# Four of seven stage-1 groups of two batches take one shared maximum, raised on GpSimd, in an attention-and-gated-FFN kernel

## The chip, the cores and the metric

The kernel runs on one core of a Trainium2 chip. The metric is device time in microseconds (us) of one execution; less is better. Before the change three runs gave 723.48, 723.59 and 724.96 us, median 723.59 us.

## What is computed

For each of 4 batches, x has 12416 rows of 128 numbers. Stage 1 lets 32 inducing rows attend over all the rows of x, stage 2 lets every row of x attend over the 32 results h, and a gated feed-forward network (128 to 1536 to 128) follows.

```python
def mab(q, kv):
    s = scale * (q @ kv.transpose(0, 2, 1))
    s = s - s.max(-1, keepdims=True)
    a = np.exp(s)
    a /= a.sum(-1, keepdims=True) + 1e-09
    return a @ kv
h = mab(I, x)            # stage 1
y = mab(x, h)            # stage 2
gate = 1.0 / (1.0 + np.exp(-(y @ w_gate)))
out = (gate * (y @ w_val)) @ w_out
```

## The kernel before, in words

**Tiles.** A batch is 97 chunks of 128 rows. One chunk stands alone (group 6, "the single"), 96 make six groups of 16 (groups 0 to 5; `groups`, L48). Batches are numbered 0 to 3 here; "batches 3 and 4" of the change are numbers 2 and 3. The whole of x of a batch lies in SBUF twice, as it is (`xn`) and transposed (`xT`), each in two buffers that the batches use in turn. A batch's loads are issued by GpSimd (`x_load`, L73), its transposes are DMAs issued by SyncE (`x_transpose_dma`, L87).

**The feed-forward loop sets the pace.** Four chunks make a block of 512 rows, 97 blocks in all. The 12 slices of the hidden width are worked off in 8 steps per block, alternately two slices (even step) and one (odd step). Step t does: on TensorE the value fill v(t) and the gate fill g(t + 2) (`hidden_mm`, L847); on VectorE the product u(t) = (tanh + 1) * v (L891); on ScalarE tanh(t + 2) of the gate (`gate`, L872). The gate fill g(t + 2) uses the PSUM banks of g(t), so it waits for tanh(t); the value fill v(t) uses those of v(t - 2), so it waits for u(t - 2). Odd steps also run `project` (L912), the matmuls with `w_out`, usually 12, and once per block ScalarE copies the block's result out (L940). Each engine takes its instructions strictly in the order in which this loop writes them.

**Slots.** An even and an odd step are one slot (`t // 2`); a batch has 96 slots, and o is the slot at which a batch's blocks begin (`base`, L947). Everything else is written out by hand at slots: `at(slot, make)` puts a piece behind the even step, `late=True` behind the odd step (`beside`, L981). While the loop works on batch b, the slots of that batch hold most of stage 2 of batch b and stage 1 of batch b + 1:

- `plan_stage1` (L287), one group of batch b + 1: at slot `score` four matmuls into one PSUM bank and VectorE's maximum over it (L222); at `score + 1`, late, ScalarE's exp (L235) with the negated maximum as bias; at `score + 2` a DMA transpose of the weights; at the three slots of `total` the sum over the rows in two halves (L270, 32 matmuls in all, into PSUM) and ScalarE's copy of the sum into `hst` (L285). Each group keeps a maximum and a sum of its own.
- `plan_combine` (L376): at `lead` VectorE's minimum over the negated maxima (L384) and `join_min` (L355), eleven small GpSimd steps that end in `top`; at `weights` ScalarE's exp over the seven maxima with `top` as bias (L389, tile `w`); one slot later GpSimd's weighted sum of the seven group sums (`join`, L393); later h and its products with the gate and value matrices.
- `plan_stage2` (L577), one group: scores at `score` and `score + 1`, ScalarE's copy to SBUF at `take` (late, L480), then GpSimd's maximum by a tree of subtract, clamp, add (`s2_lower_pool`, L482; tiles `rise` and `top`); ScalarE's exp at `weigh` (late, L504); GpSimd's sum at `weigh + 1` (L512), reciprocal and spread to `a2n` at `weigh + 3` (L536 to L558); the DMA transpose to `a2r` at `weigh + 8` (L569), which the group's first fills read.

All scores, sums and the like of stages 1 and 2 use one PSUM bank in turn, tag "m": the next user's matmuls wait until the last reader of the one before has done.

For batches b = 1 and 2 as the loop has them (so stage 1 of batches 2 and 3), the slots before are, relative to o: scores of groups 0 to 5 at 8, 12, 24, 28, 40, 44 and of the single at 32; sums at 15/16, 18/19, 31, 35, 47/48, 50/51 and 43; the combine at 52 (`lead`) and 55 (`weights`).

Of the kernel before, what the change touches and what calls it, by code (L numbers as in the profile page):

```python
# [9 lines left out]
F32 = mybir.dt.float32  # L10
F16 = mybir.dt.float16
BF16 = mybir.dt.bfloat16
AF = mybir.ActivationFunctionType
ALU = mybir.AluOpType
AX = mybir.AxisListType

AFTER = mybir.DependencyInfo(mybir.DependencyClass.Sync, mybir.DependencyReason.DATA)
P = 128
GC = 16
BC = 4  # L20
NEG = 1.0e30
TINY = 1.0e-9 / P


@with_exitstack
def kernel(
# [9 lines left out]
    nc = tc.nc  # L36
    B, N, C = x.shape
    m = inducing.shape[0]
# [4 lines left out]
    NG = NCH // GC  # L43
# [43 lines left out]
    def x_transpose_dma(b, s):  # L87
        c0, n = groups[s]
        xT_tile(b)
        nc.sync.dma_start(  # L90
            xT[b][:, c0 : c0 + n, :],
            xn[b][:, c0 : c0 + n, :].rearrange("p j c -> p (j c)"),
            transpose=True,
        )
# [66 lines left out]
    arrival = [0, NG] + list(range(1, NG))  # L161
    at_col = {s: p for p, s in enumerate(arrival)}
    EARLY = NS - 3
    nml = const.tile([P, 1 + NS - EARLY], F32, tag="nml")
    l1l = const.tile([P, 1 + NS - EARLY], F32, tag="l1l")
    nm1s = [const.tile([P, NS], F32, name=f"nm1_{q}", tag=f"nm1_{q}") for q in range(2)]
# [23 lines left out]
    def at(slot, make, late=False):  # L190
        plan.setdefault((slot, late), []).append(make)


    def s1_col(b, s):
        p = at_col[s]
        if b == 0 and p >= EARLY:
            return nml, l1l, slice(1 + p - EARLY, 2 + p - EARLY)
        return nm1s[b % 2], None if b else l1s, slice(p, p + 1)
# [58 lines left out]
    def s1_turn_dma(b, s, a1T):  # L257
        a1 = s1p.tile([P, 4, P], F16, tag="a1")
        nc.sync.dma_start(a1[:], a1T[:], transpose=True)
        return a1  # L260

    def s1_sum_pe(b, s, a1, hp, k0, k1):
        c0, n = groups[s]
        ng, w, R = s1_dims(s)
        for k in range(k0, min(k1, w)):
            for cols, src in ((slice(0, C), None), (slice(C, C + 1), ones16[:])):
                for g in range(ng):
                    if b == 0 and src is not None:
                        continue
                    nc.tensor.matmul(  # L270
                        hp[32 * g : 32 * g + 32, cols],
                        a1[:, k, 32 * g : 32 * g + 32],
                        xn[b][:, c0 + g * w + k, :] if src is None else src,
                        start=(k == 0 and src is None),
                        stop=(k == w - 1),
                        skip_group_check=True,
                    )

    def s1_sum_keep(b, s, hp):
        ng, w, R = s1_dims(s)  # L280
        width = C + 1 if b else C
        summed[b] += 1
        if b == 0 and at_col[s] >= EARLY:
            return hp[:, 0:C]
        nc.scalar.copy(out=hsts[b % 2][0:R, at_col[s], 0:width], in_=hp[0:R, 0:width])  # L285

    def plan_stage1(b, s, score, total):  # L287
        st = {}
        full = groups[s][1] == GC

        def begin():
            st["s1"] = s1_score(b, s, "m")

        def weigh():
            st["a1T"] = s1_exp(b, s, st["s1"])

        def turn():
            if full:
                st["a1"] = s1_turn_dma(b, s, st["a1T"])
            else:  # L300
                st["a1"] = s1_turn_copy(s, s1_turn_pe(b, s, st["a1T"]))

        at(score, begin)
        at(score + 1, weigh, late=full)
        at(score + 2, turn)
        first, second, keep = total

        def part(k0, k1):
            if k0 == 0:
                st["hp"] = ps.tile([P, C + 1], F32, tag="m", name="hp_ps")  # L310
            s1_sum_pe(b, s, st["a1"], st["hp"], k0, k1)

        at(first, lambda: part(0, 2))
        at(second, lambda: part(2, 4))
        at(keep, lambda: s1_sum_keep(b, s, st["hp"]))


    hT16 = {}
# [2 lines left out]
    def add_tree(x, k, out=None):  # L321
        while k > 1:
            r = k // 2
            o = x[:, 0:r] if k > 2 or out is None else out
            nc.gpsimd.tensor_tensor(out=o, in0=x[:, 0:r], in1=x[:, k - r : k], op=ALU.add)
            k -= r
# [49 lines left out]
    def plan_combine(b, lead, weights, fill):  # L376
        q = b % 2
        nm1, hst = nm1s[q], hsts[q]
        st = {}

        def least():
            assert summed[b] == NS
            ml = bp.tile([P, 1], F32, tag="ml")
            nc.vector.tensor_reduce(out=ml[:], in_=nm1[:], axis=AX.X, op=ALU.min)  # L384
            st["col"] = join_min(bp, ml)

        def weigh():
            st["w"] = bp.tile([P, NS], F32, tag="w1", name="w1")
            nc.scalar.activation(  # L389
                out=st["w"][:], in_=nm1[:], func=AF.Exp, bias=st["col"][:], scale=-1.0  # L390
            )

        def join():  # L393
            hx = bp.tile([P, NS, C + 1], F32, tag="hx", bufs=1)
            nc.gpsimd.tensor_tensor(
                out=hx[:],
                in0=hst[:],
                in1=st["w"][:].unsqueeze(2).to_broadcast((P, NS, C + 1)),
                op=ALU.mult,
            )  # L400
            add_tree(hx, NS)
            e32l = bp.tile([P, m], F32, tag="e32l")
            nc.gpsimd.tensor_scalar(
                out=e32l[:],
                in0=e32[:],
                scalar1=hx[:, 0, C : C + 1],
                scalar2=TINY,
                op0=ALU.mult,
                op1=ALU.add,
            )  # L410
            st["hx"], st["e32l"] = hx, e32l

        def total():
            lh = ps.tile([P, 2, m], F32, tag="m", name="lh_ps")
            nc.tensor.matmul(lh[:, 0, :], ones[:], st["e32l"][:], start=True, stop=True)
            nc.tensor.matmul(lh[:, 1, :], st["hx"][:, 0, 0:C], e32[:], start=True, stop=True)
            st["lh"], st["li"] = lh, l_inverse(lh[:, 0, :])

        def part(hf):
            st["hw_ps"] = hw_fill(b, hf, "m")  # L420

        def keep(hf):
            if hf == 0:
                st["hwt"] = bp.tile([P, NI, P], F16, tag="hw", bufs=B, name="hwt")
            hw_take(st["hwt"], hf, st["hw_ps"])
            if hf == 1:
                hw[b] = st["hwt"]

        at(lead, least)
        at(weights, weigh)  # L430
        at(weights + 1, join)
        at(weights + 8, total)
        at(weights + 9, lambda: h_take(b, st["lh"][:, 1, :], st["li"]))
        for hf, (first, second) in enumerate(fill):
            at(first, lambda hf=hf: part(hf))
            at(second, lambda hf=hf: keep(hf), late=True)
# [511 lines left out]
    for b in range(B):  # L948
        o = base[b]
        more = b + 1 < B  # L950

        if b == 0:
            plan_stage2(0, groups[1][0], o, None, o + 3, soon=True)
            plan_stage2(0, groups[2][0], o + 5, o + 7, o + 18)
        for s in range(3 if b == 0 else 2, NG - 1):
            k = o + 16 * s - 28
            plan_stage2(b, groups[s][0], k, k + 2, k + (14 if more else 10))
        plan_stage2(b, groups[NG - 1][0], o + 56, o + 58, o + 66, far=o + 52)
        if not more:
            continue  # L960
        early = (
            [(9, (16, 17, 17)), (13, (23, 23, 23))]
            if b == 0
            else [(8, (15, 16, 17)), (12, (18, 19, 19))]
        )
        later = [(24, (31, 31, 31)), (28, (35, 35, 35)), (40, (47, 48, 49)), (44, (50, 51, 51))]
        for s, (score, total) in enumerate(early + later + [(32, (43, 43, 43))]):
            plan_stage1(b + 1, s, o + score, [o + e for e in total])
        plan_combine(b + 1, o + 52, o + 55, [(o + 72, o + 74), (o + 80, o + 82)])
        plan_stage2(b + 1, groups[0][0], o + 67, o + 70, o + 78)  # L970
        plan_stage2(b + 1, groups[1][0], o + 84, o + 86, o + 94)
        for g in range(NS):
            when = 3 * g if b else (5, 7, 17, 19, 22, 25, 20)[g]
            at(o + when, lambda b=b, g=g: x_transpose_dma(b + 1, g))
            if b == 0 and 3 <= g < NG:
                at(o + 12, lambda g=g: x_load(1, g))
        if b + 2 < B:
            for g in range(NG):
                at(o + (28 if b == 0 else 24, 33, 42, 60, 60, 82)[g], lambda b=b, g=g: x_load(b + 2, g))

    def beside(slot, late):  # L981
        for make in plan.pop((slot, late), ()):
# [53 lines left out]
```

## Time and profile before

| what | value |
|---|---|
| median of 3 runs | 723.59 us |
| the profiled execution's own time | 723.41 us |
| its span in the trace | 721.6 us |
| granted TensorE clock | 0.999 |
| GpSimd busy in the span | 420.3 us, 58% |
| maxima of stage 1 on VectorE, 128 x 512, batches 1 to 3 | 21, mean 681 ns |
| DMA | 65.21 MB, mean 90 GB/s |

The profile counts an engine as busy from the start of an instruction to its end; on VectorE and ScalarE the next one may start some 0.07 to 0.13 us before the end of the last, so that durations add up to more than the time that passes. What an instruction costs its engine is the distance from its start to the next one's start. The 1.8 us between the span and the execution's time are taken as fixed.

### The profile page before, as it was taken

What the parts mean: (1) busy time and instruction counts of PE and PEld (TensorE: products, weight loads), DVE (VectorE), ACT (ScalarE), POOL (GpSimd) and SP (SyncE); (2) the same over time, 40 slices, a digit from 0 to 9 for tenths busy, and PEclk for the clock granted to TensorE, in tenths of its full rate; (3) what the DMA queues carried; (4) which work ended last, traced back from release to release, by engine and by line L of the source; (5) the groups of instructions that cost most, each with busy time, mean ns of one, the idle gap of its engine ahead of it and who ended that gap; (6) DMA issues with size and microseconds to landing.
All of it is one profiled execution on the core that took longest, in us unless ns stands there. A gap on an engine that the chain in (4) does not pass through costs nothing.

```text
span 721.6 us, 21567 instructions
## 1 busy us (share of the span) xinstructions
PE 645.2 (89%) x8478; PEld 390.9 (54%) x8478; DVE 703.6 (98%) x871; ACT 674.2 (93%) x1008; POOL 420.3 (58%) x699
## 2 busy tenths in 40 slices
PE   7889889999998998999989988999999899898887
PEld 4555555555555555555555555555555555555555
DVE  4799999999999999999999999999999999999998
ACT  4699999999999999999999999999999999999996
POOL 4464753888653747588666366398856665636200
PEclk9999999999999999999999999999999999999999
DMA  8879935243668344236378432220232122121211
GB/s 172 171 138 171 181 82 109 74 90 76 89 131 164 78 104 93 57 81 127 60 119 154 100 76 61 58 75 31 76 74 59 45 60 69 51 60 45 62 45 46
DMA packets 116726, 65.21 MB, mean 90 GB/s; under 512 B 99824, under 2 KB 101008, under 8 KB 116624
## 3 DMA queue, kind: packets, MB, share of 16 engines
q1 hardware_dynamic: 111936, 49.81, 31.6%
q0 software_dynamic: 4416, 13.90, 10.8%
q8 instruction: 66, 1.08, 0.6%
q14 instruction: 36, 0.29, 0.2%
q10 hardware_dynamic: 272, 0.13, 0.1%
HBM read 27.80 MB, written 25.43 MB: 74 GB/s over the span
## 4 chain that ended last, share of the span: by engine, by line
DVE 53%; issue 22%; PE 13%; ACT 8%; DMA 2%; DVEq 1%; POOL 0%; ACTq 0%; POOLq 0%
DVE u L891 51%; ACT t L878 7%; PE acc_ps L922 6%; PE v_ps L859 5%; DMA xn<-in_x_dram 2%; DVE nm L222 2%; DVEq L891 1%; PE hp_ps L270 1%; PE g_ps L859 0%; POOL xn L81 0%; PE s_ps L210 0%; ACT hwt L351 0%; PE s_ps L443 0%; PE aT_ps L248 0%; ACT a1T L235 0%
## 5 line engine op out<-in xcount | busy, mean ns | idle before, releaser
L891 DVE SCALAR_TENSOR_TENSOR u<-t,v_ps 128x512 f16<-128x512 f16 (+1 forms) x778 | 675.0, 942 | 1.6 <-PE g_ps L859 0.7
L878 ACT ACTIVATE t<-g_ps 128x512 f16<-128x512 f32 (+1 forms) x777 | 593.5, 818 | 28.2 <-ACT t L878 16.8
L859 PE MATMUL v_ps<-a2r,hwt 32*128 32x512 f16 (+1 forms) x1188 | 293.4, 371 | 66.2 <-DVE u L891 65.5
L922 PE MATMUL acc_ps<-wo,u 128*128 128x128 f16 x4656 | 327.4, 220 | 0.0
L922 PEld LDWEIGHTS <-u 128*128 128x128 f16 x4656 | 261.0, 98 | 88.0 <-issue 86.9
L859 PE MATMUL g_ps<-a2r,hwt 32*128 32x512 f16 (+1 forms) x1188 | 296.5, 377 | 0.0
L859 PEld LDWEIGHTS <-hwt 32*128 32x128 f16 x2424 | 90.9, 91 | 197.8 <-issue 153.0
L512 POOL TENSOR_TENSOR sum<-e 128x256 f32<-128x256 f16 (+1 forms) x23 | 15.5, 672 | 143.0 <-ACT e L504 139.3
L558 POOL TENSOR_TENSOR a2n<-e,rs 128x2048 f16<-128x2048 f16 (+3 forms) x25 | 86.8, 3475 | 5.4 <-DVE rs L530 2.4
L536 POOL TENSOR_TENSOR near<-sme,minus 128x16 f32<-128x16 f32 (+1 forms) x22 | 65.2, 2965 | 1.8
L940 ACT ACTIVATE o<-acc_ps 128x512 f32<-128x512 f32 x96 | 58.1, 605 | 0.0
L491 POOL TENSOR_SCALAR rise<-rise 128x256 f32<-128x256 f32 (+6 forms) x110 | 51.2, 466 | 9.7
L490 POOL TENSOR_TENSOR rise<-sc 128x256 f32<-128x256 f32 (+1 forms) x22 | 16.2, 738 | 38.6 <-ACT sc L480 38.4
L492 POOL TENSOR_TENSOR top<-top,rise 128x128 f32<-128x128 f32 (+3 forms) x88 | 28.4, 323 | 7.3
L512 POOL TENSOR_TENSOR sum<-sum 128x128 f32<-128x128 f32 (+3 forms) x92 | 28.5, 309 | 7.2
L490 POOL TENSOR_TENSOR rise<-top 128x128 f32<-128x128 f32 (+3 forms) x88 | 27.3, 311 | 6.9
L495 POOL TENSOR_TENSOR sc<-sc,top 128x512 f32<-128x512 f32 (+1 forms) x22 | 23.9, 1086 | 1.7
L443 PEld LDWEIGHTS <-xT 128*128 128x128 f16 x388 | 13.1, 96 | 11.7 <-issue 11.3
L81 POOL DMA_DIRECT2D xn<-in_x_dram x25 | 14.7, 595 | 6.3 <-DMA xn<-in_x_dram 5.5
L443 PE MATMUL s_ps<-hT,xT 128*128 128x32 f16 x388 | 18.1, 178 | 0.1
L235 ACT ACTIVATE a1T<-s_ps,nm 128x512 f16<-128x512 f32 (+1 forms) x25 | 15.7, 629 | 1.8 <-DVE nm L222 1.8
L492 POOL TENSOR_TENSOR top<-sc,rise 128x256 f32<-128x256 f32 (+1 forms) x22 | 16.2, 738 | 1.8
(132 smaller groups left out, 234.5 us busy)
## 6 DMA issues: line engine op xcount, KB each, us to landing
out_dram<-o SPq DMA_DIRECT2D x96, 256.0 KB, 2.3
xn<-in_x_dram POOLq DMA_DIRECT2D x19, 512.0 KB, 8.1
xn<-in_x_dram POOLq DMA_DIRECT2D x4, 544.0 KB, 5.8
a2r<-a2n SPq DMA_TRANSPOSE x29, 4.5
xn<-in_x_dram POOLq DMA_DIRECT2D x1, 384.0 KB, 14.5
wg<-in_moe_w_gate_dram POOLq DMA_DIRECT2D x1, 384.0 KB, 16.0
wv<-in_moe_w_val_dram POOLq DMA_DIRECT2D x1, 384.0 KB, 16.3
wo<-in_moe_w_out_dram POOLq DMA_DIRECT2D x1, 384.0 KB, 15.8
```

Of the source, the lines that this page charges most:

```text
L443: nc.tensor.matmul(s2[:, j, :], xT[b][:, c + j, :], hT16[b][:], start=(j == 0), stop=whole and j == j1 - 1, skip_group_check=True,)
L490: nc.gpsimd.tensor_tensor(out=r, in0=far, in1=near, op=ALU.subtract)
L491: nc.gpsimd.tensor_scalar_max(out=r, in0=r, scalar1=0.0)
L492: nc.gpsimd.tensor_tensor(out=top[:, 0:n, 0:w], in0=near, in1=r, op=ALU.add)
L512: nc.gpsimd.tensor_tensor(out=d[:, 0:n, :], in0=src[:, :, 0:w], in1=src[:, :, w : 2 * w], op=ALU.add)
L536: nc.gpsimd.tensor_tensor(out=near[:, 0:n], in0=sme[:, 0:n], in1=minus1[:, 0:n], op=ALU.pow)
L558: eng.tensor_tensor(out=a2n[:, 0:n, :, :], in0=e.unsqueeze(2).to_broadcast((P, n, 4, m)), in1=rs.unsqueeze(2).unsqueeze(3).to_broadcast((P ...
L859: st[what + "end"] = nc.tensor.matmul(pt[:, k, col : col + nb * P], hw[b][r : r + 32, j // 2, :], a2r[r : r + 32, o : o + nb, :].rearrange ...
L878: st["tanh"] = nc.scalar.activation(out=st["t"][:, :, c:e], in_=st["g"][:, :, c:e], func=AF.Tanh, scale=0.5)
L891: u = nc.vector.scalar_tensor_tensor(out=st["u"][:, :, c:e], in0=st["t"][:, :, c:e], scalar=1.0, in1=st["v"][:, :, c:e], op0=ALU.add, op1= ...
L922: nc.tensor.matmul(acc[0][(i // 2) % len(acc[0])][:, i, :], st["u"][:, k, ts(i, P)], wo16[:, NI * (j % 2) + j // 2, :], start=(j == 0 and ...
L940: nc.scalar.mul(out=o32[:], in_=acc[0][0][:], mul=0.5)
```

## The change

It concerns stage 1 of batches 2 and 3 alone. Groups 2, 3 and the single keep their own maxima. Groups 0, 1, 4 and 5 (`SHARED`) are scored into PSUM without VectorE's maximum; ScalarE copies the scores to SBUF (`keep`), into the first 32 chunks of the current batch's `xT`, which stage 2 no longer needs by then; GpSimd raises an elementwise maximum over the four (`lift`: subtract, clamp, add on 128 x 512, three times), folds it to 256 and 128 columns, and one VectorE reduction of 128 x 128 gives the shared negated maximum (`low`). ScalarE's exp then reads the copies in SBUF. Since the maximum is shared, the sums of two groups add up in one PSUM bank, and two copies to `hst` take the place of four; the combine has five parts, not seven. The transposes of `x`, the loads and the combine are moved to other slots.

```diff
+    SHARED = (0, 1, 4, 5)
+    NSH = NS - len(SHARED) + 2
+    shared_col = {2: 0, NG: 1, 3: 2}
...
+    def plan_shared(b, o, takes, tops, least, weighs, sums):
+        st = {}
+        nm, hst = nm1s[b % 2], hsts[b % 2]
+
+        def place(i):
+            c = NLO + 8 * i
+            return xT[b - 1][:, c : c + 8, :].rearrange("p j t -> p (j t)").bitcast(F32)
+
+        def score(i):
+            st["s1"] = s1_score_pe(b, SHARED[i], "m")
+
+        def keep(i):
+            nc.scalar.copy(out=place(i), in_=st["s1"][:])
+
+        def rise(near, far, w):
+            top, r = place(4)[:, 0:w], place(5)[:, 0:w]
+            nc.gpsimd.tensor_tensor(out=r, in0=far, in1=near, op=ALU.subtract)
+            nc.gpsimd.tensor_scalar(
+                out=r, in0=r, scalar1=BIG, scalar2=0.0, op0=ALU.min, op1=ALU.max
+            )
+            nc.gpsimd.tensor_tensor(out=top, in0=near, in1=r, op=ALU.add)
+
+        def lift(i):
+            rise(place(0) if i == 1 else place(4), place(i), 512)
+            if i == len(SHARED) - 1:
+                for w in (256, 128):
+                    rise(place(4)[:, 0:w], place(4)[:, w : 2 * w], w)
+
+        def low():
+            nc.vector.tensor_reduce(
+                out=nm[:, NSH - 2 : NSH - 1],
+                in_=place(4)[:, 0:128],
+                axis=AX.X,
+                op=ALU.max,
+                negate=True,
+            )
+            nc.gpsimd.tensor_copy(out=nm[:, NSH - 1 : NSH], in_=nm[:, NSH - 2 : NSH - 1])
+
+        def weigh(i):
+            st["a1T"] = s1p.tile([P, 512], F16, tag="a1T", name="a1T")
+            nc.scalar.activation(
+                out=st["a1T"][:], in_=place(i), func=AF.Exp, bias=nm[:, NSH - 2 : NSH - 1]
+            )
+
+        def turn(i):
+            st[i] = s1_turn_dma(b, SHARED[i], st["a1T"])
+
+        def part(i):
+            if i % 2 == 0:
+                st["hp"] = ps.tile([P, C + 1], F32, tag="m", name="hp_ps")
+            s1_sum_pe(b, SHARED[i], st[i], st["hp"], 0, 4, i % 2 == 0, i % 2 == 1)
+
+        def hold(k):
+            summed[b] += 1
+            nc.scalar.copy(out=hst[:, NSH - 2 + k, :], in_=st["hp"][:])
+
+        for i in range(len(SHARED)):
+            at(o + takes[i], lambda i=i: score(i))
+            at(o + takes[i], lambda i=i: keep(i), late=True)
+            at(o + weighs[i], lambda i=i: weigh(i), late=True)
+            at(o + weighs[i] + 1, lambda i=i: turn(i))
+            at(o + sums[i], lambda i=i: part(i))
+        for i, slot in enumerate(tops):
+            at(o + slot, lambda i=i: lift(i + 1))
+        at(o + least, low)
+        for k in range(2):
+            at(o + sums[2 * k + 1] + 1, lambda k=k: hold(k))
...
-        plan_stage2(b, groups[NG - 1][0], o + 56, o + 58, o + 66, far=o + 52)
+        late = 2 if more and b else 0
+        plan_stage2(b, groups[NG - 1][0], o + 56, o + 58, o + 66, far=o + 52 + late)
...
+        single = (32, (43, 43, 43))
+        if b == 0:
...
+            turns = (5, 7, 17, 19, 22, 25, 20)
+        else:
+            parts = {2: (8, (16, 17, 17)), 3: (12, (18, 19, 19)), NG: single}
+            turns = (-14, -4, -2, 3, 1, 8, 20)
+            plan_shared(
+                b + 1, o, (-6, 2, 10, 14), (7, 11, 15), 23, (26, 30, 42, 46), (39, 40, 51, 52)
+            )
...
-        plan_combine(b + 1, o + 52, o + 55, [(o + 72, o + 74), (o + 80, o + 82)])
+        plan_combine(
+            b + 1, o + 52 + late, o + 55 + late, [(o + 72, o + 74), (o + 80, o + 82)]
+        )
...
-            when = 3 * g if b else (5, 7, 17, 19, 22, 25, 20)[g]
-            at(o + when, lambda b=b, g=g: x_transpose_dma(b + 1, g))
+            at(o + turns[g], lambda b=b, g=g: x_transpose_dma(b + 1, g))
...
-                at(o + (28 if b == 0 else 24, 33, 42, 60, 60, 82)[g], lambda b=b, g=g: x_load(b + 2, g))
+                at(o + (24 if b else 28, 33, 42, 50, 60, 68)[g], lambda b=b, g=g: x_load(b + 2, g))
```

The parts left out fit `s1_sum_pe`, `s1_sum_keep`, `s1_col` and `plan_combine` to the shared groups: start and stop flags of the sums, the columns of `nm1` and `hst`, and five parts in place of seven.

More of the change, by code (lines that the diff above doesn't have):

```diff
@@ L21 @@
 NEG = 1.0e30
+BIG = 3.0e38
 TINY = 1.0e-9 / P
@@ L191, in at, with s1_place @@
         plan.setdefault((slot, late), []).append(make)
+    def s1_place(b, s):
+        return at_col[s] if b < 2 else shared_col[s]
     def s1_col(b, s):
-        p = at_col[s]
+        p = s1_place(b, s)
         if b == 0 and p >= EARLY:
@@ L260, in s1_turn_dma, with s1_sum_pe @@
         return a1
-    def s1_sum_pe(b, s, a1, hp, k0, k1):
+    def s1_sum_pe(b, s, a1, hp, k0, k1, first=True, last=True):
         c0, n = groups[s]
@@ L273, in s1_sum_pe @@
                         xn[b][:, c0 + g * w + k, :] if src is None else src,
-                        start=(k == 0 and src is None),
-                        stop=(k == w - 1),
+                        start=(first and k == 0 and src is None),
+                        stop=(last and k == w - 1),
                         skip_group_check=True,
@@ L284, in s1_sum_keep @@
             return hp[:, 0:C]
-        nc.scalar.copy(out=hsts[b % 2][0:R, at_col[s], 0:width], in_=hp[0:R, 0:width])
+        nc.scalar.copy(out=hsts[b % 2][0:R, s1_place(b, s), 0:width], in_=hp[0:R, 0:width])
     def plan_stage1(b, s, score, total):
@@ L379, in plan_combine @@
         st = {}
+        ns = NS if b < 2 else NSH
         def least():
-            assert summed[b] == NS
+            assert summed[b] == ns
             ml = bp.tile([P, 1], F32, tag="ml")
-            nc.vector.tensor_reduce(out=ml[:], in_=nm1[:], axis=AX.X, op=ALU.min)
+            nc.vector.tensor_reduce(out=ml[:], in_=nm1[:, 0:ns], axis=AX.X, op=ALU.min)
             st["col"] = join_min(bp, ml)
@@ L389, in weigh @@
             nc.scalar.activation(
-                out=st["w"][:], in_=nm1[:], func=AF.Exp, bias=st["col"][:], scale=-1.0
+                out=st["w"][:, 0:ns],
+                in_=nm1[:, 0:ns],
+                func=AF.Exp,
+                bias=st["col"][:],
+                scale=-1.0,
             )
@@ L395, in join @@
             nc.gpsimd.tensor_tensor(
-                out=hx[:],
-                in0=hst[:],
-                in1=st["w"][:].unsqueeze(2).to_broadcast((P, NS, C + 1)),
+                out=hx[:, 0:ns, :],
+                in0=hst[:, 0:ns, :],
+                in1=st["w"][:, 0:ns].unsqueeze(2).to_broadcast((P, ns, C + 1)),
                 op=ALU.mult,
             )
-            add_tree(hx, NS)
+            add_tree(hx, ns)
             e32l = bp.tile([P, m], F32, tag="e32l")
@@ L957 @@
             plan_stage2(b, groups[s][0], k, k + 2, k + (14 if more else 10))
-        plan_stage2(b, groups[NG - 1][0], o + 56, o + 58, o + 66, far=o + 52)
+        late = 2 if more and b else 0
+        plan_stage2(b, groups[NG - 1][0], o + 56, o + 58, o + 66, far=o + 52 + late)
         if not more:
             continue
[L961 to L964, printed above, removed]
-        )
-        later = [(24, (31, 31, 31)), (28, (35, 35, 35)), (40, (47, 48, 49)), (44, (50, 51, 51))]
-        for s, (score, total) in enumerate(early + later + [(32, (43, 43, 43))]):
-            plan_stage1(b + 1, s, o + score, [o + e for e in total])
-        plan_combine(b + 1, o + 52, o + 55, [(o + 72, o + 74), (o + 80, o + 82)])
+        single = (32, (43, 43, 43))
+        if b == 0:
+            early = [(9, (16, 17, 17)), (13, (23, 23, 23))]
+            later = [(24, (31, 31, 31)), (28, (35, 35, 35)), (40, (47, 48, 49)), (44, (50, 51, 51))]
+            parts = dict(enumerate(early + later + [single]))
+            turns = (5, 7, 17, 19, 22, 25, 20)
[5 more added lines that the diff above has]
+            )
+        for s, (score, total) in parts.items():
+            plan_stage1(b + 1, s, o + score, [o + e for e in total])
+        plan_combine(
+            b + 1, o + 52 + late, o + 55 + late, [(o + 72, o + 74), (o + 80, o + 82)]
+        )
         plan_stage2(b + 1, groups[0][0], o + 67, o + 70, o + 78)
```

## The prediction, on record before the result

> **What bounds the kernel now.** I read the page first: who is busy.
>
> ```profile
> PE 645.2 (89%) x8478; PEld 390.9 (54%) x8478; DVE 703.6 (98%) x871; ACT 674.2 (93%) x1008; POOL 420.3 (58%) x699
> L891 DVE SCALAR_TENSOR_TENSOR u<-t,v_ps 128x512 f16<-128x512 f16 (+1 forms) x778 | 675.0, 942 | 1.6 <-PE g_ps L859 0.7
> ```
>
> VectorE is busy 98% of the span and idles 1.6 us before all 778 products together. So VectorE is the bound, as long as nothing makes it wait. Next, the busy times over the stretches in which the loop works on batches 1, 2 and 3:
>
> ```profile
> 203.37:373.84 170.47, 154.25 (x2057) 93.55 (x2057) 170.46 (x204) 164.66 (x246) 110.56 (x184) 1.00 0.49 99
> 373.84:544.31 170.47, 154.27 (x2057) 93.56 (x2057) 170.46 (x204) 164.66 (x246) 107.07 (x178) 1.00 0.35 79
> 544.31:710.50 166.19, 148.89 (x1814) 89.43 (x1814) 166.19 (x193) 157.62 (x226) 75.85 (x117) 1.00 0.20 56
> ```
>
> Columns: length, then PE, PEld, DVE, ACT, POOL. Batch 3 has no stage 1 beside it: 166.19 us, or 1.731 us for each of its 96 slots. Batches 1 and 2 take 4.28 us more, and VectorE has 11 more instructions there: stage 1 costs just what it puts on VectorE.
>
> **What the change takes from VectorE.** The timeline of VectorE around a maximum:
>
> ```profile
> 216.60 1.81 DVE L891 SCALAR_TENSOR_TENSOR u<-t,v_ps 128x512 f16<-128x512 f16 x2
> 218.33 0.68 DVE L222 TENSOR_REDUCE nm<-s_ps 128x1 f32<-128x512 f32 x1
> 218.93 3.53 DVE L891 SCALAR_TENSOR_TENSOR u<-t,v_ps 128x512 f16<-128x512 f16 x4
> ```
>
> A maximum holds VectorE from 218.33 to 218.93, 0.60 us. Two batches lose four each: 8 * 0.60 = 4.8 us. Each gets one reduction of 128 x 128 back. Its nearest row takes 0.29 us, some 0.08 of it under the next instruction, as with the maximum (0.68 against 0.60); I take 0.20 us, with 0.15 and 0.30 as ends. **Gain 4.4 us**, if VectorE stays fed.
>
> ```profile
> L779 DVE TENSOR_REDUCE nmx_a<-s_ps 128x4 f32<-128x128 f32 x1 | 0.3, 291 | 0.4 <-PE s_ps L443 0.4
> ```
>
> ScalarE gets four copies of 0.59 us per batch and loses two short ones. At 164.66 of 170.47 us it has room for that. Its tanh runs ahead of VectorE, and it fits single pieces of that length between the tanhs today without VectorE waiting, so I cost the copies themselves at nothing. What costs is who waits behind a piece.
>
> **Wait 1: the bank "m" handed over from a late piece.** At slot 39 the sum of shared groups 0 and 1 begins; at slot 38, late, stands ScalarE's copy of stage 2's scores, out of the same PSUM bank. TensorE waits there, and behind the sum stand the next fills. The kernel before has this very pair once, in batch 0 (copy at 22 late, sum at 23):
>
> ```profile
> 71.58 3.67 DVE L891 SCALAR_TENSOR_TENSOR u<-t,v_ps 128x1024 f16<-128x1024 f16 x4
> ...
> 73.01 0.59 ACT L480 COPY sc<-s_ps 128x512 f32<-128x512 f32 x1
> 73.66 0.24 PE L270 MATMUL hp_ps<-xn,a 128*32 128x128 f16 x4 [0.41 <-ACT sc L480]
> 74.08 0.39 PE L859 MATMUL v_ps<-a2r,hwt 32*128 32x512 f16 x1
> 74.39 0.84 PE L922 MATMUL acc_ps<-wo,u 128*128 128x128 f16 x12
> 75.17 0.39 PE L859 MATMUL v_ps<-a2r,hwt 32*128 32x512 f16 x2
> 75.50 0.40 PE L210 MATMUL s_ps<-xT,indT 128*32 128x512 f16 x4
> 75.62 1.22 DVE L891 SCALAR_TENSOR_TENSOR u<-t,v_ps 128x1024 f16<-128x1024 f16 x1 [0.36 <-PE g_ps L859]
> 75.83 0.38 PE L859 MATMUL v_ps<-a2r,hwt 32*128 32x512 f16 x1
> ```
>
> Four products from 71.58 should end two slots later, at 75.04; the fifth starts at 75.62. That is **0.58 us** of VectorE. The rows also price TensorE's work: a sum of 32 matmuls holds it 73.66 to 74.08, 0.42 us; a score 75.50 to 75.83, 0.33; a fill pair 0.32 (75.17 to 75.50, 74.08 to 74.39); a project 0.78 (74.39 to 75.17). A slot without extras is 0.32 + 0.32 + 0.78 = 1.42 of 1.73 us, so 0.31 us is free per slot. A whole sum overruns that by 0.11, a score by 0.02. A sum alone, at slot 31 of batch 1:
>
> ```profile
> 257.67 4.77 DVE L891 SCALAR_TENSOR_TENSOR u<-t,v_ps 128x1024 f16<-128x1024 f16 x5
> 262.36 0.27 DVE L222 TENSOR_REDUCE nm<-s_ps 32x1 f32<-32x128 f32 x1
> ```
>
> Five products (1.13 and 0.60 in turn, together 1.73 a slot) take 4.59; here 4.69: 0.10. So per batch: slot 39 0.58; slot 40, a second whole sum with no slack left, 0.11; slots 51 and 52 0.10 + 0.11; scores at -6 and 2 0.03 together. The sums at 31 and 35 go: they gave back 0.10 and about 0.01.
>
> The scores at 10 and 14 stand behind ScalarE's exp of groups 2 and 3 at 9 and 13, late, same bank. Today's rows there:
>
> ```profile
> 220.60 0.68 ACT L235 ACTIVATE a1T<-s_ps,nm 128x512 f16<-128x512 f32 x1
> 220.79 0.39 PE L859 MATMUL v_ps<-a2r,hwt 32*128 32x512 f16 x2
> ```
>
> TensorE would reach the score at 220.79 + 0.32 = 221.11; the exp ends at 221.28, and a wait ends 0.06 later (73.60 to 73.66 above). It waits 0.23 and works 0.33: 0.56 less 0.31 free and 0.02 = **0.23 us** each, 0.46 a batch. Wait 1 in all: 0.69 + 0.21 + 0.03 + 0.46 - 0.11 = **1.28 us a batch**.
>
> **Wait 2: the combine, moved by two slots.** GpSimd and ScalarE around slots 52 to 58 of batch 1:
>
> ```profile
> 296.00 0.66 POOL L512 TENSOR_TENSOR sum<-e 128x256 f32<-128x256 f16 x1 [9.64 <-ACT e L504]
> 298.66 0.85 POOL L358 COPY quad<-ml 32x1 f32<-32x1 f32 x4
> 300.44 0.83 POOL L373 COPY top<-quad 32x1 f32<-32x1 f32 x4
> 301.36 2.94 POOL L536 TENSOR_TENSOR near<-sme,minus 128x16 f32<-128x16 f32 x1
> 305.28 3.61 POOL L558 TENSOR_TENSOR a2n<-e,rs 128x2048 f16<-128x2048 f16 x1
> 303.51 0.29 ACT L389 ACTIVATE w<-nm,top 128x7 f32<-128x7 f32 x1
> 303.70 2.13 ACT L878 ACTIVATE t<-g_ps 128x512 f16<-128x512 f32 x3
> 304.29 6.40 DVE L891 SCALAR_TENSOR_TENSOR u<-t,v_ps 128x1024 f16<-128x1024 f16 x7
> 308.21 0.84 PE L922 MATMUL acc_ps<-wo,u 128*128 128x128 f16 x12
> 309.01 0.39 PE L859 MATMUL v_ps<-a2r,hwt 32*128 32x512 f16 x2
> ```
>
> Today `join_min` (slot 52) stands ahead of stage 2's reciprocal and spread (slot 53) in GpSimd's queue: `top` is ready at 301.27, the exp `w` (slot 55) runs at 303.51. The change moves `join_min` to 54, behind the spread, and `w` to 57. Then the reciprocal starts at 298.66 and the spread ends 7.53 us later (301.36 to 308.89), at 306.19; `join_min`, 2.6 us long, ends at 308.85. ScalarE comes to `w` near 307.0 (two slots, 3.46 us, after 303.51), and behind `w` stands the tanh of step 117, the odd step of slot 58. It starts at 308.85 + 0.06 + 0.19 = 309.10 and ends at 309.69. The gate fill g(119) waits for it until 309.75, and behind it stand in TensorE's queue a project and v(118): 309.75 + 0.32 + 0.80 (308.21 to 309.01) + 0.39 + 0.06 = 311.32 for u(118). Unhindered, u(118) comes three slots after 304.29, at 309.48, plus the 0.21 lost at 51 and 52 before it: 309.69. **1.6 us a batch.** If `w` found `top` in time it would be nothing; the upper end is 2.0, with the copy at 58 adding to it.
>
> **What I cost at nothing.** GpSimd gets three lifts and two folds a batch, hidden as long as group 2's `a2r` lands before slot 31. Its rows:
>
> ```profile
> L491 POOL TENSOR_SCALAR rise<-rise 128x256 f32<-128x256 f32 x18 | 15.5, 860 | 1.6
> L491 POOL TENSOR_SCALAR rise<-rise 128x128 f32<-128x128 f32 x18 | 9.5, 526 | 1.6
> L490 POOL TENSOR_TENSOR rise<-sc 128x256 f32<-128x256 f32 x18 | 13.2, 731 | 27.8 <-ACT sc L480 27.8
> L490 POOL TENSOR_TENSOR rise<-top 128x128 f32<-128x128 f32 x18 | 8.2, 455 | 1.4
> 223.37 1.08 POOL L495 TENSOR_TENSOR sc<-sc,top 128x512 f32<-128x512 f32 x1
> 244.39 3.61 POOL L558 TENSOR_TENSOR a2n<-e,rs 128x2048 f16<-128x2048 f16 x1
> DMA to landing us min/median/max: 2.4/4.5/10.8
> ```
>
> On the slope from 128 to 256 columns, 512 takes 1.29 (subtract or add) and 1.53 us (clamp); with some 0.09 between them a lift is 4.4, the folds 2.6 + 1.7. From 224.45 (end of stage 2's tree) that ends at 242.0; sum (2.6, as from 296.00 to 298.66) and spread (7.5) of group 2 end at 252.1 instead of 248.0, and `a2r` lands 4.5 later, 256.6. Slot 31 begins at 259.40 today (257.67 and a slot), after the change about 258.7 (two maxima less, 0.46 more of Wait 1), its gate fill 0.47 earlier (309.01 against 309.48) at 258.2: **1.6 us to spare**. VectorE's reduction at slot 23 comes near 246, 4 us behind the folds. The new slots of transposes and loads leave 6 slots or more before each use, over 10 us against landings of 4.5.
>
> [...]
>
> **The sum.** 723.41 - 4.4 + 2 * (1.28 + 1.6) = 724.8 us against the profiled execution's own time; the median of the runs shown stands 0.18 higher, so I forecast **724.9 us**: the gain is eaten, **no change** within 0.2% (1.45 us, about what a measurement can tell from no change), a little on the slow side.
>
> **Rivals.**
> - *The gain comes whole*, both waits absorbed by leads I read too small: 723.41 - 4.4 - 0.2 = 718.8. For it: VectorE stalls almost nowhere today. Against it: the row at 73.66. 0.12.
> - *The combine does not block ScalarE*: 724.8 - 3.2 = 721.6. Against it: queues keep the written order, as the rows at 298.66 to 301.36 show. 0.12.
> - *The bank waits are absorbed* and the combine's is not: about 722.9. 0.10.
> - *GpSimd is late (slower).* Place: slot 31. It decides once lifts and folds take 1.6 us more than 17.5. If the clamp's second operation doubled its slope, that is 5.0 us more a batch, 3.4 beyond the margin: 724.8 + 6.8 = 731.6; half of it, 727 to 728. For it: no row shows 512 columns with two operations; nothing but the slope prices them. 0.18.
> - My forecast, 0.48, spans 723.9 to 725.8: the ends of Wait 2 and of the reduction.
>
> Below 722 lie the first rival and most of the second, 0.20. Above 724.86 (profiled clock) lie the fourth and a good 0.2 of the forecast: 0.39. Within: 0.41. The range 720.8 to 728.0 leaves out the first rival and the upper part of the fourth, 0.2.
>
> **What would show it.** VectorE's 128 x 512 maxima fall from 21 to 13. The waits list a sum waiting for ScalarE's copy of `sc` twice more, scores waiting for `a1T` four times, and `w` waiting some 1.8 us for `top`, twice. The two 170.47 us stretches end within 1 us of that; products wait for TensorE some 6 us in all. Wrong would be: stretches of 168 us (no waits), a `w` that finds `top` ready, or fills waiting for `a2r`.

## The result, and the profile after

The changed kernel takes **727.53 us** (median of 6 runs, 726.78 to 729.71) against 723.66 us before, a ratio of 1.0055 with a 95% interval of 1.0039 to 1.0071. It is slower by half a per cent: inside the range of the prediction, 2.6 us above its point, beyond the 0.2% that it had called no change, and beyond the 723.9 to 725.8 us that it had given to its own forecast among the rivals. The profiled execution took 726.80 us, 1.8 of them outside its span of 725.0.

The page of the changed kernel first, then its busy times over the stretches of batches 1, 2 and 3 (length, then PE, PEld, DVE, ACT, POOL, granted clock, DMA share, GB/s):

```profile
PE 649.0 (90%) x8478; PEld 393.5 (54%) x8478; DVE 702.0 (97%) x865; ACT 676.9 (93%) x1012; POOL 442.6 (61%) x731
L972 DVE SCALAR_TENSOR_TENSOR u<-t,v_ps 128x512 f16<-128x512 f16 (+1 forms) x778 | 677.2, 942 | 6.6 <-PE g_ps L940 4.0
```

```profile
203.87:375.50 171.63, 155.69 (x2057) 94.62 (x2057) 169.57 (x202) 165.87 (x248) 121.97 (x200) 1.00 0.48 99
375.50:547.48 171.98, 156.19 (x2053) 94.84 (x2053) 169.36 (x202) 165.37 (x247) 118.43 (x194) 0.99 0.32 72
547.48:713.91 166.43, 149.20 (x1814) 89.61 (x1814) 166.35 (x193) 157.67 (x225) 75.65 (x117) 1.00 0.20 56
```

VectorE has less to do (702.0 us, not 703.6) and idles more. The idle column (6.6 us ahead of products) understates it, since a product that starts 0.08 us late still overlaps the end of the one before; so I also took the distances between the starts of all products. The stretches of batches 1 and 2 grew from 170.47 us to 171.63 and 171.98. Batch 2's mean clock of 0.99 is new. The waits name the culprits (us in total, times, longest):

```profile
DVE u L972 <- PE g_ps L940: 4.0, 8, 1.0
ACT w L466 <- POOL top L449: 2.5, 2, 1.3
PE g_ps L940 <- ACT t L959: 2.4, 3, 1.1
PE hp_ps L277 <- ACT sc L561: 1.2, 3, 0.4
```

The second line did not exist before, the fourth stood at 0.4 us, once. Slot 58 of batch 1 in the timeline, the place of Wait 2:

```profile
308.54 0.30 ACT L466 ACTIVATE w<-nm,top 128x5 f32<-128x5 f32 x1 [1.27 <-POOL top L449]
308.74 1.98 ACT L959 ACTIVATE t<-g_ps 128x512 f16<-128x512 f32 x3
309.35 0.69 DVE L972 SCALAR_TENSOR_TENSOR u<-t,v_ps 128x512 f16<-128x512 f16 x1 [0.36 <-ACT t L959]
309.37 0.37 PE L940 MATMUL g_ps<-a2r,hwt 32*128 32x512 f16 x1 [1.08 <-ACT t L959]
309.67 0.84 PE L1003 MATMUL acc_ps<-wo,u 128*128 128x128 f16 x12
310.45 0.39 PE L940 MATMUL v_ps<-a2r,hwt 32*128 32x512 f16 x2
310.89 1.82 DVE L972 SCALAR_TENSOR_TENSOR u<-t,v_ps 128x1024 f16<-128x1024 f16 x2 [0.86 <-PE g_ps L940]
```

That is the forecast chain link by link: `w` waits for `top`, the odd tanh behind it ends late, the gate fill waits for the tanh, the project and the even value fill stand behind the gate fill, and the even product comes last. In batch 2 the same event has a sequel; here is TensorE (first number after the length) and its clock (1.00, then 0.50) in four stretches of 3.40 us, the length of the spell:

```profile
475.30:478.70 3.40, 3.40 (x54) 2.29 (x52) 3.40 (x6) 3.21 (x5) 3.15 (x6) 1.00 0.00 0
478.70:482.10 3.40, 2.13 (x26) 1.01 (x25) 2.49 (x4) 2.15 (x6) 2.62 (x8) 1.00 1.09 229
482.10:485.50 3.40, 3.40 (x28) 1.75 (x23) 2.44 (x3) 2.58 (x5) 2.97 (x6) 0.50 0.04 10
485.50:488.90 3.40, 3.01 (x37) 1.75 (x36) 3.40 (x5) 3.36 (x6) 2.90 (x7) 1.00 0.21 77
```

After a stretch in which TensorE was busy for 2.13 of 3.40 us, its granted clock stands at 0.50 from 482.1 to 485.5. A project of 12 matmuls takes 1.46 us there (from 482.82), not 0.84, and VectorE, fed more slowly, does 2.44 us of work in that stretch. The same block in batch 1 of the same execution has no such sequel: TensorE was busy for 2.33 us there, and the clock stayed at 1.00 in the stretch behind it.

```profile
308.01:311.42 3.41, 2.33 (x27) 1.14 (x26) 2.20 (x3) 2.88 (x6) 2.75 (x6) 1.00 0.85 160
311.42:314.84 3.42, 2.77 (x34) 1.53 (x32) 3.42 (x5) 3.36 (x6) 2.99 (x6) 1.00 0.03 7
```

The forecast's other wait, at slot 39, on VectorE:

```profile
271.46 4.26 DVE L972 SCALAR_TENSOR_TENSOR u<-t,v_ps 128x512 f16<-128x512 f16 x5
276.08 3.06 DVE L972 SCALAR_TENSOR_TENSOR u<-t,v_ps 128x1024 f16<-128x1024 f16 x3 [0.37 <-PE g_ps L940]
```

Five products that begin with an odd one take 3 * 0.60 + 2 * 1.13 = 4.06 us undisturbed; the sixth comes after 4.62. The 0.56 us are those of the twin in batch 0 (0.58). At slot 10, the score of the shared group starts 0.06 us after the end of group 2's exp (221.12 + 0.68 = 221.80), as forecast:

```profile
221.12 0.68 ACT L242 ACTIVATE a1T<-s_ps,nm 128x512 f16<-128x512 f32 x1
221.86 0.40 PE L217 MATMUL s_ps<-xT,indT 128*32 128x512 f16 x4
```

One loss is in none of the lists of long waits. At slots 26, 30, 42 and 46 stands the shared groups' exp; ScalarE, TensorE and VectorE after the first of them:

```profile
252.28 0.72 ACT L365 ACTIVATE a1T<-xT,nm 128x512 f16<-128x512 f32 x1
252.89 3.06 ACT L959 ACTIVATE t<-g_ps 128x1024 f16<-128x1024 f32 x4
253.84 0.39 PE L940 MATMUL v_ps<-a2r,hwt 32*128 32x512 f16 x2
253.96 0.39 PE L940 MATMUL g_ps<-a2r,hwt 32*128 32x512 f16 x2
250.85 5.36 DVE L972 SCALAR_TENSOR_TENSOR u<-t,v_ps 128x1024 f16<-128x1024 f16 x6
```

The gate fill usually starts with the value fill; here it starts 0.12 later, since it waits for the tanh before it. An even product waits, by a dependency that the kernel declares itself (L901 to L906 of the kernel before), not for its tanh but for the gate fill behind that tanh. Six products take 5.27 us to the end of the last one (3 * 1.13 + 3 * 0.60, and 0.08 by which the last outlasts its 0.60), here 5.36: by the starts of the products 0.08 lost, four times a batch.

### The profile page after: what moved, and what is told of

The parts are those of the page before. It is cut to its first block, busy times and chain, and to the rows that moved or that the text cites. A ratio compares the mean times of both kernels' runs of the same rounds, so it can differ in the third digit from the quotient of the medians.

```text
span 725.0 us, 21608 instructions
## 1 busy us (share of the span) xinstructions
PE 649.0 (90%) x8478; PEld 393.5 (54%) x8478; DVE 702.0 (97%) x865; ACT 676.9 (93%) x1012; POOL 442.6 (61%) x731
## 4 chain that ended last, share of the span: by engine, by line
DVE 49%; issue 21%; PE 14%; ACT 8%; POOL 4%; DMA 3%; DVEq 1%; ACTq 0%; POOLq 0%
DVE u L972 47%; ACT t L959 7%; PE acc_ps L1003 6%; PE v_ps L940 5%; DMA xn<-in_x_dram 2%; POOL a2n L639 1%; DMA a<-a1T 1%; PE hp_ps L277 1%; POOL near L617 1%; DVEq L972 1%; PE g_ps L940 1%; DVE nm L229 1%; POOL sum L593 1%; PE s_ps L217 0%; ACT a1T L242 0%
## 5 line engine op out<-in xcount | busy, mean ns | idle before, releaser
L940 PEld LDWEIGHTS <-hwt 32*128 32x128 f16 x2424 | 92.4, 91 | 193.6 <-issue 148.0
L277 PE MATMUL hp_ps<-xn,a 128*32 128x128 f16 x388 | 13.2, 221 | 1.6 <-ACT sc L561 1.2
```

The source lines that it names most:

```text
L940: st[what + "end"] = nc.tensor.matmul(pt[:, k, col : col + nb * P], hw[b][r : r + 32, j // 2, :], a2r[r : r + 32, o : o + nb, :].rearrange ...
```

## The experiments

The theory after the result: VectorE's gain is real; the bank handovers and the combine take it back as forecast; to them come the exps, a half-speed spell of TensorE behind the combine's block, and a late transpose in batch 0. The rival: TensorE and ScalarE are so near their own bounds that the gain is lost wherever the pieces are put.

**w one slot later.**

```diff
-        at(weights, weigh)
+        at(weights + (1 if b > 1 else 0), weigh)
```

> The changed kernel with the combine's exp w one slot later, at 58, where top is ready; nothing else is moved. Theory (w blocks ScalarE, and TensorE's idling behind it halves its clock): the stalls of VectorE at slot 58 of batches 1 and 2 (1.38 and 2.11 us in the changed kernel's profile) go, the half-speed spell near 482 us goes with them, span 725.0 - 3.5 = 721.5, time about 723.3, and the granted clock is 0.999 in every run, with runs within 1 us of each other. Rival (the time lies in the bank handovers and in the exps; the block at 58 is taken back later): time above 725.5, the spread of some 3 us between runs stays.

Measured: 723.65 us (10 runs, median), ratio to before 0.9996 (0.9985 to 1.0007), the clock 1.000 in its profile. Its batches 1 and 2:

```profile
204.06:374.45 170.39, 155.69 (x2057) 94.83 (x2057) 169.51 (x202) 165.87 (x249) 121.96 (x200) 1.00 0.49 100
374.45:544.45 170.00, 155.02 (x2053) 94.45 (x2053) 169.20 (x202) 165.38 (x247) 118.44 (x194) 1.00 0.32 73
```

One instruction in each of the two batches, moved by one slot, is worth 3.9 us by the medians and 3.0 by the profiled executions (726.80 and 723.80); a stall of 0.15 us a batch stays at 59. Nine of the ten runs lie between 723.45 and 723.80 us. The rival, that the block is taken back later, is out. What is left of the change then takes as long as the kernel before: the gain and the other waits cancel.

**The late combine alone, in the kernel before.**

```diff
-        plan_combine(b + 1, o + 52, o + 55, [(o + 72, ...
+        late = 2 if b else 0
+        plan_combine(b + 1, o + 52 + late, o + 55 + late, [(o + 72, ...
```

> The kernel before with one part of the change alone: the combine of batches 2 and 3 starts at slot 54 and its exp stands at 57, in place of 52 and 55. Theory (the order in GpSimd's queue, join_min behind the spread, costs by itself): 1.4 to 2.1 us a batch, time 726.2 to 728.0, granted clock below 0.999 in most runs. Rival (the block exists only because stage 1 of the changed kernel loads the engines): time within 0.7 us of before, 723.0 to 724.4.

Measured: 728.65 us (5 runs, 727.41 to 730.87), ratio 1.0064 (1.0041 to 1.0087). Its batches, a wait, and two stretches around slot 58 of batch 1:

```profile
203.53:376.42 172.89, 155.77 (x2057) 94.32 (x2057) 170.82 (x205) 164.71 (x247) 110.28 (x184) 0.99 0.48 97
376.42:550.55 174.13, 157.34 (x2057) 95.40 (x2057) 171.00 (x205) 164.81 (x247) 106.80 (x178) 0.98 0.34 77
```

```profile
ACT w L389 <- POOL top L373: 2.6, 2, 1.4
```

```profile
308.40:311.80 3.40, 2.13 (x27) 1.16 (x26) 2.00 (x3) 2.90 (x6) 2.82 (x5) 0.99 0.81 151
311.80:315.20 3.40, 3.40 (x31) 2.13 (x30) 3.10 (x4) 2.71 (x5) 2.97 (x6) 0.50 0.03 7
```

The order in GpSimd's queue is enough by itself to lose 2.4 us in batch 1 and 3.7 in batch 2, more than the expected 1.4 to 2.1; the median lies above the expected 728.0 too. Here a half-speed spell comes in both batches, and in batch 2 it lasts for two stretches:

```profile
479.02:482.43 3.41, 2.40 (x31) 1.34 (x28) 3.21 (x4) 2.25 (x5) 2.45 (x12) 1.00 0.74 118
482.43:485.85 3.42, 3.25 (x23) 1.70 (x23) 1.37 (x2) 2.63 (x5) 3.18 (x4) 0.50 0.52 115
485.85:489.26 3.41, 3.41 (x33) 2.27 (x31) 2.87 (x4) 2.40 (x4) 3.02 (x5) 0.50 0.02 5
```

Together with `w` one slot later this settles Wait 2: the cause is `join_min` behind the spread, with `w` standing too early for it.

**The sums at 40 and 41.**

```diff
-                ... (26, 30, 42, 46), (39, 40, 51, 52)
+                ... (26, 30, 42, 46), (40, 41, 51, 52)
```

> The changed kernel with the sums of shared groups 0 and 1 at slots 40 and 41 in place of 39 and 40. Theory (the sum waits for the PSUM bank that ScalarE's copy at 38 late still reads): the stall of 0.57 us at slot 39 goes; 0.09 and 0.11 stay at 40 and 41; gain 0.46 us a batch. Rival (TensorE has too little room for two whole sums in a row, wherever they stand): stalls of 0.4 us or more at 40 and 41.

Measured, by the starts of the products: nothing at 39, 0.08 at 40, 0.10 at 41, so the bank was the cause. But slot 43 rises from 0.08 to 0.26 us. The copy of the sum now stands at 42, beside the exp at 42 late and the single's copy at 43; that this is why was not tested. Net gain 0.3 us a batch (0.49 less 0.18), not 0.46. The one run took 728.0 us at a granted clock of 0.998: in its trace the loop starts 1.4 us later than in the changed kernel's, and slot 58 of batch 1 loses 2.4 us with a half-speed spell behind it.

**The product waits for its own tanh.** Only in the four slots with an exp, batches 1 and 2:

```diff
+        free = t // 192 in (1, 2) and t // 2 % 96 in (28, 32, 44, 48)
-        if st["cnt"] == 2 and 4 <= t < NST - 2:
+        if st["cnt"] == 2 and 4 <= t < NST - 2 and not free:
```

> The changed kernel; in slots 28, 32, 44 and 48 of batches 1 and 2 the even product waits for its own tanh, not for the gate fill that follows that tanh. Theory (the exps of the shared groups at 26, 30, 42 and 46 delay a tanh, and the product loses 0.08 us because it waits on for the gate fill behind that tanh): the eight stalls of 0.08 us go, 0.66 us in all. [...]

Measured: the stalls fall from 0.08 to 0.04 us, and one of 0.04 appears at 49. Half of the theory holds; what the other 0.04 waits for stays open. (One run, 729.35 us; in its trace the clock stands at 0.50 for 6.8 us behind slot 58 of batch 1 and for 3.4 behind that of batch 2.)

**The scores behind the odd step.**

```diff
+            behind = i > 1
-            at(o + takes[i], lambda i=i: score(i))
-            at(o + takes[i], lambda i=i: keep(i), late=True)
+            at(o + takes[i], lambda i=i: score(i), late=behind)
+            at(o + takes[i] + (1 if behind else 0), lambda i=i: keep(i), late=not behind)
```

> The changed kernel with the scores of groups 4 and 5 behind the odd step of slots 10 and 14, and their copies to SBUF one slot later. Theory (the score waits for the exp of groups 2 and 3, which reads the same bank): the stalls of 0.22 us at 10 and 14 fall to 0.05 or less, 0.35 us a batch or more. Rival (the score itself is too long for TensorE's room in that slot): 0.2 us or more stay. The stalls at slot 58 stay in either case.

Measured (one run, 728.85 us): 0.28 us at 10 and 14, not 0.05, and 0.17 more at 16. The theory failed here, and the rival's sign came. TensorE at slot 10:

```profile
223.28 0.37 PE L941 MATMUL v_ps<-a2r,hwt 32*128 32x512 f16 x1 [0.20 <-DVE u L973]
223.60 0.40 PE L217 MATMUL s_ps<-xT,indT 128*32 128x512 f16 x4
223.93 0.84 PE L1004 MATMUL acc_ps<-wo,u 128*128 128x128 f16 x12
224.71 0.39 PE L941 MATMUL v_ps<-a2r,hwt 32*128 32x512 f16 x2
```

The score no longer waits for its bank, but TensorE's 0.31 us of room in a slot lie in two places: 0.20 ahead of the odd value fill (the bracket) and 0.1 ahead of the even one. Behind the odd step only the second is left, and the score's 0.33 us overrun it by 0.2.

**Batch 0's loads back.**

```diff
-   at(o + (24 if b else 28, 33, 42, 50, 60, 68)[g], ...
+   at(o + (24 if b else 28, 33, 42, 50 if b else 60, 60, 68 if b else 82)[g], ...
```

> The changed kernel with batch 0's loads of groups 3 and 5 for batch 2 back at slots 60 and 82. Theory (the load at 50, which GpSimd issues 116 us into the span, delays the landing of the transposed weights for the sum at slot 50 of batch 0): the stall of 0.33 us or more at slot 50 of batch 0 goes, and that transpose lands within 5 us. Rival (the wait there comes from the transpose being issued later or from something else): the stall stays.

Measured (one run, 727.54 us): the stall at slot 50 of batch 0 is gone, and the transpose lands 4.6 us after its issue, as in the kernel before. In the changed kernel it was issued at nearly the same time (116.66, before 116.50), but behind two loads, not one, and landed after 7.1 us:

```profile
115.38 1.18 POOL L82 DMA_DIRECT2D xn<-in_x_dram  x2
```

```profile
123.80 0.24 PE L277 MATMUL hp_ps<-xn,a 128*32 128x128 f16 x4 [0.33 <-DMA a<-a1T]
```

**Three maxima of each batch left out, in the kernel before.** Groups 1, 4 and 5 of batches 2 and 3 are shifted by group 0's maximum, which GpSimd copies into their columns; their own maxima are not computed.

```diff
+        if b > 1 and s in (1, 4, 5):
+            nc.gpsimd.tensor_copy(out=nm[:, col], in_=nm[:, 0:1])
+            return
```

> The kernel before; in batches 2 and 3 the maxima of groups 1, 4 and 5 are left out, and these groups are shifted by group 0's maximum (GpSimd copies its column). Six VectorE maxima fewer, no other piece is moved. Theory (a maximum is worth its 0.60 us on VectorE): 6 * 0.60 = 3.6 us less, minus up to 0.6 where the exp now finds no lead (0.08 each) and a score no cover, so 720.1 to 720.7. Rival (other engines are so close behind that VectorE's time does not come out): above 722.

Measured: 721.97 us, ratio 0.9979 (0.9970 to 0.9989): 1.7 us gained, neither 3.6 nor nothing.

```profile
203.44:373.13 169.69, 155.25 (x2057) 93.97 (x2057) 169.22 (x201) 164.34 (x246) 110.93 (x187) 1.00 0.50 99
373.13:542.47 169.34, 154.90 (x2057) 93.78 (x2057) 168.97 (x201) 164.13 (x246) 107.38 (x181) 1.00 0.35 79
```

The stretches of batches 1 and 2 shrink by 0.78 and 1.13 us where three maxima are 1.80. In both, the trace has a stall of 0.20 us at each of the slots 14, 42 and 46, behind the exps that lost their maximum (batch 1 has 0.35 more, at 18, 19 and 71). The reading that fits: while VectorE takes a maximum, ScalarE gains 0.60 us of lead, and the exp that follows spends it; without the maximum the exp makes the next product late. A maximum removed is worth 0.40 us at such a place, not 0.60.

**All waits moved.** w at 58, scores behind the odd step, products waiting for their own tanh, loads back, sums in halves at 39 late, 40, 41, 41 and 50 to 53.

> The changed kernel with every wait found so far taken out by slots: w at 58; scores of groups 4 and 5 behind the odd step at 10 and 14, their copies one slot later; the sums of the shared groups in halves at 39 late, 40, 41, 41 and 50, 51, 52, 53; the even products at 28, 32, 44 and 48 waiting for their own tanh; batch 0's loads of groups 3 and 5 back at 60 and 82. Theory (VectorE's 4.4 us are real, and the handovers, the combine and the late transpose of batch 0 eat them): per batch 0.4 (10, 14), 0.5 (39 to 41), 0.2 (51, 52) and 0.2 (exps) less than with w at 58 alone, 0.45 less in batch 0, so 723.65 - 3.1 = 720.5, with 720.0 to 721.2. Rival (the gain is taken back wherever the work is put, since TensorE and ScalarE are near their own bounds): 722.5 or more.

Measured: 722.56 us, ratio 0.9979 (0.9969 to 0.9990): faster than both kernels, but 2.1 us short of the theory, and just within what the rival had named. The largest stalls left are 0.28 + 0.28 + 0.17 a batch at 10, 14 and 16, 0.29 at 39 to 41, 0.16 at 59.

**The same, with scores and sums where TensorE has room.**

```diff
-            behind = i > 1
+            behind = False
-                ((39, True), (40, False), (41, False), (41, False),
+                ((40, False), (40, False), (41, False), (41, False),
```

> As the version with all waits moved, but the scores of groups 4 and 5 stand behind the even step again at 10 and 14, with their copies late in the same slot, and the sums of groups 0 and 1 are whole at 40 and 41, held at 41. Theory (TensorE's room in a slot is split, some 0.2 us ahead of the odd fill and 0.1 ahead of the even one, so work behind the odd step costs more): per batch 0.45 instead of 0.56 at 10 and 14, nothing instead of 0.17 at 16, 0.18 instead of 0.29 at 39 to 41: 0.4 a batch less, 721.5 to 722.1. Rival (the place in the slot makes no difference, the amount of work does): 722.4 to 722.8, as before this edit.

Measured: **721.88 us**, ratio 0.9969 (0.9958 to 0.9981), as expected, and the best version here; the 0.45 at 10 and 14 are still in it. Of VectorE's 4.4 us, 1.8 have come out (723.67 to 721.88). So the rival that the gain is lost wherever the pieces are put is refuted for these 1.8 us; whether other slots would bring out the rest was not tried.

## Why the prediction was right and wrong, point by point

- **VectorE's gain, 4.4 us: right.** The stretches of batches 1 and 2 grew by 1.16 and 1.51 us, while the stalls between products grew by 3.36 and 3.71: the difference is 2.20 a batch, as forecast.
- **Wait 1: right.** Forecast and measured, a batch: 0.69 and 0.67 at 39 and 40; 0.46 and 0.44 at 10 and 14; 0.21 and 0.20 at 51 and 52.
- **Wait 2: the mechanism was right, its size was cut off too early.** Forecast 1.6; measured 1.38 in batch 1, where `w` waited 1.27 us for `top` and not 1.8, and 2.11 in batch 2, where the half-speed clock adds to it. The prediction followed the block to the first product and stopped; the spell behind it, with TensorE's clock at 0.50 for 3.4 us in batch 2, was not priced.
- **What the prediction put at nothing was the step that failed,** first of all ScalarE, in the reason "fits single pieces of that length between the tanhs today without VectorE waiting". The copies did cost nothing; the shared groups' exps, which had no term of their own, cost 0.08 us four times a batch, 0.33. The pieces that fit today hold ScalarE for 0.46 to 0.55 us (in the kernel before 273.33 to 273.79, 218.62 to 219.10 and 659.95 to 660.49), or follow a maximum; the shared groups' exp holds ScalarE for 0.61 (252.28 to 252.89) and no maximum goes ahead of it.
- **"The new slots of transposes and loads leave 6 slots or more" looked at their own uses alone.** In batch 0, which I had not looked at, the load moved to slot 50 held up the transpose of stage 1's weights: 0.33 us at slot 50.
- **The sum.** The profiled execution came out 2.0 us above the 724.8: the exps 0.66, batch 0 0.50, Wait 2 0.29, and some 0.57 of small stalls in batches 1 and 3; Wait 1 came out 0.1 smaller. Batch 0 starts 0.2 us later, and pairs of stalls of 0.08 and 0.16 us come up in places without any edit (slots 70 and 71 of batch 1, 12 and 13 of batch 3; elsewhere in other kernels). Their cause stays open.
- **The median stands 0.7 us above the profiled execution,** 0.2 before. The six runs spread over 3 us, with granted clocks of 0.994 to 0.998, and with w at 58 nine of ten lie within 0.4. I read that as half-speed spells that differ from run to run, though the changed kernel's trace shows one run alone; they are not all of the spread, since the run of 728.49 us had a clock of 0.998. The kernel before has single runs with a lower clock too (726.21 us at 0.998, beside a median of 723.64).
- **That the time lies inside the range is luck in part.** The range reached up to 728 for the rival in which GpSimd is late, and that rival did not come; the time went beyond 725.8 by what the prediction had put at nothing.
- **The signs.** The maxima fell to 13, the sum waited for `sc` twice more, `w` waited for `top` twice, and no fill waited for `a2r`. That the two stretches end within 1 us of 170.47 failed (1.16 and 1.51 more). The scores' waits for `a1T` stand in no list of waits; the rows of slot 10 above show one.
- **The rivals.** That GpSimd would be late has fallen: by GpSimd's timeline, a lift took 3.4 us with gaps (224.93 to 228.31), not 4.4, and the folds were done at 238.6, not 242.0. That the combine doesn't block ScalarE was refuted by the wait of `w` and by the first two experiments, that the bank waits are absorbed by the sums at 40 and 41.

```profile
224.93 1.26 POOL L341 TENSOR_TENSOR xT<-xT 128x512 f32<-128x512 f32 x1
228.31 1.27 POOL L341 TENSOR_TENSOR xT<-xT 128x512 f32<-128x512 f32 x1
238.13 0.45 POOL L345 TENSOR_TENSOR xT<-xT 128x128 f32<-128x128 f32 x1
```

The groups of the changed kernel by shape (busy us, mean ns of one):

```profile
L229 DVE TENSOR_REDUCE nm<-s_ps 128x1 f32<-128x512 f32 x13 | 8.9, 682 | 0.7 <-PE s_ps L217 0.7
L341 POOL TENSOR_TENSOR xT<-xT 128x512 f32<-128x512 f32 x6 | 7.6, 1267 | 0.3
L342 POOL TENSOR_SCALAR xT<-xT 128x512 f32<-128x512 f32 x6 | 3.7, 613 | 0.5
L342 POOL TENSOR_SCALAR xT<-xT 128x256 f32<-128x256 f32 x2 | 0.8, 399 | 0.2
L365 ACT ACTIVATE a1T<-xT,nm 128x512 f16<-128x512 f32 x8 | 5.8, 722 | 0.0
```

The maxima fell to 13. The subtraction took the 1.27 us that the slope gave (1.29); the clamp took 0.61, not 1.53.

## What to carry to other kernels

When a piece is moved in a queue, look at what it is now queued behind on the engine that feeds it, and follow the block to the end, through the queues of all engines. At slot 58 of batch 1 each queue kept its written order: GpSimd's spread (302.35) ahead of `join_min` (305.91), ScalarE's `w` (308.54) ahead of the tanh (308.74), TensorE's gate fill (309.37) ahead of the project (309.67); so 1.27 us of waiting for `top` became 0.36 of VectorE's at the odd product (309.35) and 0.86 at the even one (310.89). A bound engine's work can be another engine's time to catch up: with three maxima left out, one of 0.60 us was, by the reading above, worth 0.40 at slots 14, 42 and 46. Before you remove it, ask who lived on it. A piece has to fit the place in the slot where the room lies; the slot's free time as a whole does not tell: of 0.31 us, 0.20 lay ahead of the odd value fill and 0.1 ahead of the even one, and with the scores behind the odd step, 0.33 us each, the second was overrun by 0.2.

## What the runs showed that I had not expected

- **TensorE's granted clock fell to 0.50 behind stretches in which it was busy for more than half of the time.** A stretch of 3.40 us in which it was busy 2.13 (both in the changed kernel and with the late combine alone) is followed by 0.50 for one stretch of 3.40; with w at 58 no such spell comes in the trace, and the clock stays 1.00. The busy time by the profile does not decide it alone: 2.40 of 3.41 us were followed by half speed (late combine, batch 2), 2.33 of 3.41 were not (changed kernel, batch 1). What does decide it stays open.
- **The clamp with two operations was faster on GpSimd than the one with one.** The change's minimum and maximum over 512 columns took 613 ns, and 399 over 256; stage 2's maximum alone over 256 columns takes 860 in the kernel before. Why was not tested.
